# Moving the residual sums, the bias product and the LN2 tails from GpSimd to VectorE in a fused transformer block

## The chip, the core and the metric

The kernel runs on one core of one Trainium2 chip. A core has five engines with a queue of instructions each: PE (TensorE, matrix products into PSUM; PEld stands for its weight loads), DVE (VectorE), ACT (ScalarE), POOL (GpSimd) and SP (SyncE, which here issues the DMAs). Each engine works through its own queue in order and waits, at its head, until semaphores tell that the operands are there and the buffers free. The metric is the time of one execution in microseconds, taken as the median of several runs.

## What is computed

One block with adaptive layer norm: a modulation vector from a condition c, a local attention (16 heads of 28, each query looks at 8 keys, two rows apart), and an MLP. x has 2048 rows of 448 columns, F is 1792.

```python
mod = (silu(c) @ w_mod)                       # sa, ca, ga, sb, cb, gb
h = layernorm(x) * (1 + ca) + sa
x = x + ga * attention(h, wqkv, wo)
h = layernorm(x) * (1 + cb) + sb
y = layernorm(h)                              # the MLP normalises once more
x = x + gb * (gelu(y @ w1 + b1) @ w2 + b2)
```

The last line is what the change is about. The kernel scales w2 by gb once, and computes `x + gb*b2` for each block of rows apart from the product: `gbb2 = gb * b2` (one row, held on all 128 partitions), `x1p = x + gbb2`, and at the end `out = (gelu(...) @ (w2*gb)) + x1p`.

## The kernel before

The rows are cut into 8 blocks (p = 0 to 7) of 256: 128 partitions, and two neighbouring rows on each partition, so a block is a 128 x 896 tile of x. Attention runs in 9 batches (i = 0 to 8) of 228 queries, the MLP in 4 tiles (t = 0 to 3) of two blocks.

The kernel first lists all its operations as numbered tasks (`add`, line 111), each with the engine that does it, and then issues them in an order that is written out by hand: `ORDER` (line 51) holds the task numbers in sequence, with a suffix where a task runs on another engine than its first (`:D` DVE, `:A` ACT, `:P` POOL). A task that goes to an engine is queued there in that sequence. `SLOTS` (line 43) gives each buffer, in the order in which the listing creates them, its place: `P` buffers are the four slots of two PSUM banks each, and a buffer has to wait until all readers of the one before it in its slot are done.

The tasks that the change and the prediction speak of:

- Attention of batch i (line 678): V product `pv` (L706, or L548 for the later batches), its copy on ACT (L721), two logit products `lt` for two halves of the heads (L738), an exponential of each on ACT (L745), a mask product of each on DVE (L751), the sums `pd` (L760) and the attention product `po` (L771), logarithm and exponential of the sums (L780, L782), the output times the inverse sum on DVE (L788).
- q and k of blocks 2 to 7 (line 614): a product `pq` (L548, L554) for k and for q, copied (L628) and transposed by DMA (L631).
- Output projection of block p (line 797): PE product (L803), sum with x on DVE (L810), row statistics (L456, L458), inverse deviation on POOL (`rstd`, L469), normalisation (L478), two products or sums with the modulation (`h2`, L819), statistics again, inverse deviation on POOL again, normalisation to `yb`, and a *tail*: a copy of its last 64 columns per row (L485 to L492) that completes the tile for the DMA transpose `yT` (L834). Tails run on POOL unless ORDER says otherwise: before, those of blocks 0, 3, 4 and 7 run on POOL, 2 and 5 on DVE, 1 and 6 on ACT.
- `gbb2` (L657), on POOL: needs b2, whose load is L368, and gb. The scaling of w2 by gb is seven DVE tasks (L661), one for each pair of 128-row slabs of w2.
- MLP of tile t (line 845): first projection (L548, L554), gelu on ACT (L864), second projection (L883) from the scaled w2, final sum `fin` on DVE (L889), store (L893).
- `residual` (line 838): x1p, two POOL additions per block of 448 columns each (L841), and a *gate* before them (L868): a POOL copy of one element of the first gelu's result, which holds the additions back until that gelu is done.

Around the change, DVE's queue before 74 us holds row statistics and normalisations of blocks 2 and 3 mixed with the seven scalings of w2; the last scaling, of pair 0, is the one whose slab the second projection of tile 0 reads first. POOL's queue holds, in this sequence: inverse deviations, gbb2, an inverse deviation, the gate, the four additions of blocks 0 and 1, the inverse deviation of block 3, its tail. The SP queue holds the load of b2 as its last load but for transposes.

Of the kernel before, what the change touches and what calls it, by code (L numbers as in the profile page):

```python
# [10 lines left out]
BF16 = mybir.dt.bfloat16  # L11
ACT = mybir.ActivationFunctionType
ALU = mybir.AluOpType

S, D, H, DH, F = 2048, 448, 16, 28, 1792
# [5 lines left out]
NS = 2  # L21
# [33 lines left out]
105 119:A 145 143 133 100 146 121 136 134 126 148 137 107 147 7 127 149:D 122 138 124 150 129 139 190 123 191 140 198  # L55
141 128 125 200 199 269 130 271 236 40 270 207 33 209 38 241 201 35 237 208 210 185 211 154 39 153 242 202 152 212
151:A 8 203 187 213 238 204 159 239 214:D 205 215 186 240 155 278 206 188 279 280 156 160 307:R 161 281 243 37 282 272
192 273:A 162 157 189 171 308:D 194 172 283 193 244 218 173 195 163 219 158 275 284 196 216 285 167 217 286 447:P 246
197 164 168 165 228 174 169:D 274 309 312 276:D 277 220 313 310 314 166 221 229 225 230 311 224 222:D 247 170 315 245
176 317 316 175 226 248 233 232 318 227 290 249 289:A 319 43 287:A 223 288 320 234 250 558:P 46 45 559 321 47 231 253  # L60
345 342 346 251 560 303 482:P 44 252 324 343 322 291 561 254 323 325 347 326 344 292 304 255 293 327 348 328 373:R 256
305 294 329 257 350 258 375 52 378 376 330 340:R 53 333 379 235 377 374 296 334 331 300 41 295 351 332 259 49 335 380
299 341 336 337 297 260 382 262 301 381 349 263 261 264 338:A 383 483 352 339 384 265 484 266 449 353 267 485 385 268
# [3 lines left out]
402 452 404 443 487 453 370 490 454 444 436 455 371:D 372 456 434 491 405 488 457 493 445 459 458 492 460 435 494 461  # L67
# [3 lines left out]
513 547 515:D 599 516 564 602 568 481 569 570 604 603 571 546 605 572 548 606 573 628 607 608 574 549 635 575 550 609  # L71
612 636 577 630 637 578 610 629 640 576 579 638 581 639 611 613 580 582 641 631 583 633 586 651 614 632 587 584 585
616 588 642 615 648 617 654 646 647 618 634 652 645 656 621 649 619 644 622 620 623 643 658 650 625 624 589 626 664
590 655 627 591:A 653 657 439 592 659 556 665 662 663 674 666 660 661 669 667 675 668 678 676 679 677 686 672 673 671
687 681 670 680 690 691 694 697 693 682 688 692 685 695 683 689 701 684 698 696 709 699 710 702 711 712 705 700 703
706 704 707 708
# [77 lines left out]
def kernel(  # L154
# [14 lines left out]
    nc = tc.nc  # L169
# [3 lines left out]
    P = Plan()  # L173
    add = P.add

    cst = ctx.enter_context(tc.tile_pool(name="cst", bufs=1))
# [15 lines left out]
    x_all = cst.tile([128, NP, NS * D], BF16, name="x_all")  # L192
# [14 lines left out]
    ga_bc, sb_bc, g2_bc, gb_bc = [mod_bc[:, i, :] for i in range(4)]  # L207
    gbb2_bc = cst.tile([128, D], FP32, name="gbb2_bc")
    seen = cst.tile([128, 1], BF16, name="seen")
    b2_bc = cst.tile([128, D], BF16, name="b2_bc")  # L210
# [160 lines left out]
    for a in range(2):  # L371
        load(lambda a=a: nc.sync.dma_start(out=w1_r[KS * a:KS * a + KS, :],
                                           in_=B_w1[(KT - 1) * 128:D, a * F // 2:(a + 1) * F // 2]), 0.5, [f"w1r{a}"])
    for i in range(7):
        load(lambda i=i: nc.sync.dma_start(out=w2_s[:, 2 * i:2 * i + 2],
                                           in_=B_w2[256 * i:256 * i + 256].rearrange("(f p) n -> p f n", p=128)),
# [105 lines left out]
    def xn(p, n):  # L482
        return x_all[:, p, n * D:(n + 1) * D]

    def tail(zy, keys, key, head=False):  # L485
        src, dst = lambda: zy.t[:, :, DP - 2 * KS:DP - KS], lambda: zy.t[:, :, DP - KS:DP]
        if head:
            add("DVE", 0.11, lambda: nc.vector.tensor_copy(out=dst(), in_=src()), reads=keys, bufs=[zy], writes=[key], name="tail", port=True)
            return
        add("POOL", 0.35, lambda: nc.gpsimd.tensor_copy(out=dst(), in_=src()), reads=keys, bufs=[zy], writes=[key], name="tail",  # L490
            port=True, alt={"DVE": (0.12, lambda: nc.vector.tensor_copy(out=dst(), in_=src())),
                            "ACT": (0.20, lambda: nc.scalar.copy(out=dst(), in_=src()))})  # L492
# [141 lines left out]
    def mods():  # L634
# [22 lines left out]
        add("POOL", 1.05, lambda: nc.gpsimd.tensor_tensor(out=gbb2_bc[:], in0=gb_bc, in1=b2_bc[:], op=ALU.mult),  # L657
# [139 lines left out]
    def out_proj(p):  # L797
# [27 lines left out]
        yb = fixed("zy", zys)  # L825
# [3 lines left out]
        tail(yb, [(yb, 0), (yb, 1)], (yb, 2))  # L829
# [8 lines left out]
    def residual(p, gate):  # L838
        x1p = x1p_of[p] = sb("xp", [128, NS, D], FP32, "x1p")
        for n in range(NS):  # L840
            add("POOL", 1.0, lambda n=n: nc.gpsimd.tensor_tensor(out=x1p.t[:, n, :], in0=xn(p, n), in1=gbb2_bc[:], op=ALU.add),  # L841
                reads=[f"x{p}", "gbb2"], bufs=[x1p], writes=[(x1p, n)], port=True, after=[gate], name="x1p")


    def mlp(t, tbl, lts):
# [22 lines left out]
        gate = add("POOL", 0.1, lambda: nc.gpsimd.tensor_copy(out=seen[:], in_=hm.t[:, 0, 0, 0:1]), reads=[(hm, 0)], bufs=[hm], port=True, name="gate")  # L868
        residual(2 * t, gate)
        residual(2 * t + 1, gate)  # L870
        for q in range(2):
# [5 lines left out]
            for ns, c0, c1 in (([0], 0, D), ([1], 0, D // 2), ([1], D // 2, D)) if last else (([0, 1], 0, D),):  # L877
                p2, n0, n1 = psum("p2"), ns[0], ns[-1] + 1
                for n in ns:
# [11 lines left out]
                    bufs=[p2, x1p], reads=[(p2, n) for n in ns] + [(x1p, n) for n in ns], writes=[f"out{p}{n0}{c0}"] + ([] if last else [f"x{p}"]), name="fin")  # L891
# [71 lines left out]
```

## Time and profile before

| | us |
|---|---|
| median of 3 runs | 169.14 (169.13 to 170.44) |
| span of the profiled execution, first to last instruction | 166.6 |
| DMA share of the slices between 62 and 71 us | 0.9 and more |
| POOL, inverse deviations (22) | 16.7 |
| POOL, gbb2 (1) | 1.1 |
| POOL, gates (4) | 1.3 |
| POOL, tails (7, three of them of the first layer norm) | 2.5 |

How to read the views: a row of a timeline is start, duration, engine, line, operation, output and inputs, shapes and count (rows with a count are several instructions put together); in brackets stands how long the engine had been idle before and what ended that. Times count from the first instruction. "x2" rows of DVE overlap by a few hundredths, since an instruction starts before the one ahead of it has quite ended. In rows of stretches stands for each engine the busy time and the number of instructions, then the granted PE clock, the DMA share and the rate.

### The profile page before, as it was taken

The numbers are of one execution on the slowest core, as the hardware profiler recorded it, in microseconds if no ns is written. First come the engines' busy times: TensorE is split into PE (matmuls) and PEld (weight loads), VectorE is DVE, ScalarE is ACT, GpSimd is POOL, SyncE is SP. The second block draws the span as 40 slices with busy tenths as digits, with TensorE's granted clock in tenths as the row PEclk, the third lists the DMA queues.
The fourth block names the chain that finished last, engine by engine and source line by source line (L and its number), as shares of the span: only waits on it lengthen the run. The fifth ranks groups of instructions, "written<-read, shape, count | busy, mean of one in ns | idle before, by whom it ended". The sixth has DMA issues, their size and how long they took to land.

```text
span 166.6 us, 4971 instructions
## 1 busy us (share of the span) xinstructions
PE 160.9 (97%) x2126; PEld 83.7 (50%) x2126; DVE 116.1 (70%) x271; ACT 102.4 (61%) x142; POOL 46.7 (28%) x73
## 2 busy tenths in 40 slices
PE   6999899999999999999999999999999999999992
PEld 4678544444545543445555344556434455344572
DVE  6889899958899989996938886574788930500032
ACT  3378898798489953859674468947536820097300
POOL 3136332300261201289100114700002870007200
PEclk9999999999999999999999999999999999999999
DMA  5999989799999999900091000009010026110003
GB/s 152 323 335 311 182 269 172 147 160 190 222 185 306 147 161 245 151 0 6 2 139 46 4 0 0 4 0 126 8 55 0 0 55 185 64 46 0 0 1 110
DMA packets 35573, 18.78 MB, mean 113 GB/s; under 512 B 28507, under 2 KB 34592, under 8 KB 35552
## 3 DMA queue, kind: packets, MB, share of 16 engines
q1 hardware_dynamic: 35548, 18.47, 51.0%
q8 instruction: 16, 0.26, 0.7%
q14 instruction: 5, 0.04, 0.1%
q10 hardware_dynamic: 4, 0.00, 0.0%
HBM read 9.81 MB, written 1.84 MB: 70 GB/s over the span
## 4 chain that ended last, share of the span: by engine, by line
PE 88%; DMA 4%; ACT 2%; SPq 2%; POOL 1%; DVE 1%; issue 1%
PE p L883 26%; PE p L548 22%; PE pq L548 8%; PE pw L803 8%; PE pv L706 5%; PE p L554 4%; PE lt L738 4%; PE po L771 3%; PE pv L548 3%; DMA wqk_st<-in_A_wqkv_dram 3%; PE pq L554 2%; DMA kT<-zy 2%; PE pd L760 1%; SPq L349 1%; PE pb L641 1%
## 5 line engine op out<-in xcount | busy, mean ns | idle before, releaser
L864 ACT ACTIVATE hm<-p,b_col 128x512 bf16<-128x512 f32 x56 | 33.9, 692 | 29.9 <-PE p L554 27.3
L883 PE MATMUL p<-w_s,hm 128*128 128x448 bf16 (+1 forms) x238 | 44.1, 342 | 0.0
L548 PE MATMUL p<-yT,w_s 128*128 128x512 bf16 x168 | 38.1, 380 | 0.0
L469 POOL TENSOR_TENSOR rs_all<-mvs,neg_half 128x2 f32<-128x2 f32 x22 | 16.7, 764 | 58.0 <-DVE mvs L458 57.9
L883 PEld LDWEIGHTS <-hm 128*128 128x128 bf16 x238 | 22.6, 98 | 19.3 <-issue 0.8
L889 DVE TENSOR_TENSOR x_all<-p,x1p 128x896 bf16<-128x896 f32 (+2 forms) x10 | 8.9, 902 | 25.9 <-PE p L883 25.9
L548 PEld LDWEIGHTS <-w_s 128*128 128x128 bf16 x168 | 15.8, 98 | 20.9 <-issue 2.9
L456 DVE BATCH_NORM_STATS2 stt<-x_all 128x6 f32<-128x448 bf16 x32 | 18.6, 608 | 0.8 <-DMA x_all<-in_A_x_dram 0.6
L745 ACT ACTIVATE et<-lt 128x928 bf16<-128x928 f32 x18 | 16.0, 947 | 4.2 <-PE lt L738 3.9
L841 POOL TENSOR_TENSOR x1p<-x_all,gbb_bc 128x448 f32<-128x448 bf16 x16 | 17.8, 1137 | 0.0
L548 PE MATMUL pq<-wqk_st,hT 128*128 128x448 bf16 x72 | 15.0, 354 | 0.0
L788 DVE TENSOR_TENSOR qT<-po,den 128x912 bf16<-128x912 f32 x9 | 10.0, 1106 | 6.6 <-ACT den L782 6.4
L751 DVE TENSOR_TENSOR et<-et,mask 128x928 bf16<-128x928 bf16 x18 | 11.8, 683 | 3.1 <-ACT et L745 3.0
L803 PE MATMUL pw<-wo_s,qT 128*128 128x448 bf16 x64 | 13.3, 353 | 0.0
L780 ACT ACTIVATE den<-pd 128x928 f32<-128x928 f32 x9 | 8.5, 943 | 5.9 <-PE pd L760 5.7
L819 DVE TENSOR_TENSOR h<-h,mod_bc 128x896 bf16<-128x896 bf16 x16 | 11.1, 710 | 0.3
L628 ACT CAST zy<-pq 128x896 bf16<-128x896 f32 x10 | 8.9, 912 | 1.7 <-PE pq L554 0.9
L548 PEld LDWEIGHTS <-hT 128*128 128x128 bf16 x72 | 6.4, 98 | 6.9 <-issue 1.6
L782 ACT ACTIVATE den<-den,den_bias 128x928 f32<-128x928 f32 x9 | 9.6, 1072 | 0.2
L478 DVE TENSOR_SCALAR zy<-h,mvs,rs_all 128x448 bf16<-128x448 bf16 x16 | 6.6, 457 | 4.4 <-POOL rs_all L469 4.4
L810 DVE TENSOR_TENSOR x_all<-pw,x_all 128x896 bf16<-128x896 f32 x8 | 8.7, 1086 | 1.3 <-PE pw L803 1.3
L456 DVE BATCH_NORM_STATS2 stt<-h 128x6 f32<-128x448 bf16 x16 | 9.4, 612 | 0.2
(115 smaller groups left out, 182.0 us busy)
## 6 DMA issues: line engine op xcount, KB each, us to landing
w_s<-in_B_w_dram SPq DMA_DIRECT2D x7, 224.0 KB, 3.8
out_dram<-x_all SPq DMA_DIRECT2D x7, 224.0 KB, 2.1
x_all<-in_A_x_dram SPq DMA_DIRECT2D x3, 448.0 KB, 5.3
wmod<-in_w_mod_dram SPq DMA_DIRECT2D x3, 448.0 KB, 7.2
w_s<-in_B_w_dram SPq DMA_DIRECT2D x3, 448.0 KB
wqk_st<-in_A_wqkv_dram SPq DMA_DIRECT2D x3, 225.0 KB, 3.9
wm_st<-in_w_mod_dram SPq DMA_DIRECT2D x1, 672.0 KB, 4.6
x_all<-in_A_x_dram SPq DMA_DIRECT2D x2, 224.0 KB, 2.6
```

What stands on the lines that cost most here:

```text
L456: add("DVE", 0.53, lambda: nc.vector.bn_stats(out=stt[:, w, b, 0:6], in_=src()), reads=reads, bufs=bufs, after=early if w == b == 0 else ( ...
L469: ways = {"POOL": (0.55 + 0.17 * n, lambda: nc.gpsimd.tensor_tensor(out=r, in0=v, in1=neg_half[:, 0:n], op=ALU.pow))}
L548: nc.tensor.matmul(out(), lhsT=lhs(kt, slice(0, 128)), rhs=rhs(kt, slice(0, 128)), start=first and kt == 0, stop=not first and kt == KT - 2)
L554: nc.tensor.matmul(out(), lhsT=lhs(KT - 1, rows), rhs=rhs(KT - 1, rows), start=first, stop=not first, tile_position=(rows.start, 0))
L745: exps.append(add("ACT", 0.83, lambda half=half, lt=lt: nc.scalar.activation(out=et.t[:, 2 * half:2 * half + 2].rearrange("p r m c -> p r ...
L751: nc.vector.tensor_tensor(out=ev, in0=ev, in1=mask[:], op=ALU.mult)
L788: nc.vector.tensor_tensor(out=qT[:, :, LEAD + q00:LEAD + q00 + 2 * WQ], in0=po.t[:, :, 0:NS * 4 * WQ].rearrange("p j (m c) -> p m j c", c=WQ),
L803: nc.tensor.matmul(pw.t[:, s, 0:D], lhsT=qT[:, KT * s + ft, LEAD + 128 * p:LEAD + 128 * p + 128], rhs=wo_s[:, ft, :], start=(ft == 0), sto ...
L819: add("DVE", 0.55, lambda vec=vec, op=op: nc.vector.tensor_tensor(out=h2.t[:], in0=h2.t[:], in1=vec.unsqueeze(1).to_broadcast([128, NS, D] ...
L841: add("POOL", 1.0, lambda n=n: nc.gpsimd.tensor_tensor(out=x1p.t[:, n, :], in0=xn(p, n), in1=gbb2_bc[:], op=ALU.add), reads=[f"x{p}", "gbb ...
L864: gelus.append(add("ACT", 0.585, lambda f=f, a=a, p1=p1s[g]: nc.scalar.activation(out=hm.t[:, f].rearrange("p n c -> p (n c)"), in_=p1.t[: ...
L883: nc.tensor.matmul(p2.t[:, n, 0:c1 - c0], lhsT=hm.t[:, f, n, q * 128:(q + 1) * 128], rhs=w2_s[:, f, c0:c1], start=(f == parts[0][0]), stop ...
```

## The change

Four things move from POOL to DVE, and one is dropped:

- x1p of a block is one DVE addition of 896 columns (gbb2 read twice by a broadcast) instead of two POOL additions of 448;
- gbb2 is a DVE product;
- the tails of the second layer norm that were on POOL (blocks 0, 3, 4, 7) are DVE copies;
- the four gates are gone.

```diff
-    def tail(zy, keys, key, head=False):
+    def tail(zy, keys, key, head=False, late=False):
...
+        if late:
+            add("DVE", 0.12, lambda: nc.vector.tensor_copy(out=dst(), in_=src()), reads=keys, bufs=[zy], writes=[key], name="tail",
+                port=True, alt={"ACT": (0.20, lambda: nc.scalar.copy(out=dst(), in_=src()))})
+            return
...
-        add("POOL", 1.05, lambda: nc.gpsimd.tensor_tensor(out=gbb2_bc[:], in0=gb_bc, in1=b2_bc[:], op=ALU.mult),
+        add("DVE", 0.5, lambda: nc.vector.tensor_tensor(out=gbb2_bc[:], in0=gb_bc, in1=b2_bc[:], op=ALU.mult),
...
-        tail(yb, [(yb, 0), (yb, 1)], (yb, 2))
+        tail(yb, [(yb, 0), (yb, 1)], (yb, 2), late=True)
...
-    def residual(p, gate):
+    def residual(p):
         x1p = x1p_of[p] = sb("xp", [128, NS, D], FP32, "x1p")
-        for n in range(NS):
-            add("POOL", 1.0, lambda n=n: nc.gpsimd.tensor_tensor(out=x1p.t[:, n, :], in0=xn(p, n), in1=gbb2_bc[:], op=ALU.add),
-                reads=[f"x{p}", "gbb2"], bufs=[x1p], writes=[(x1p, n)], port=True, after=[gate], name="x1p")
+        add("DVE", 1.0, lambda: nc.vector.tensor_tensor(out=x1p.t[:], in0=x_all[:, p, :].rearrange("p (s d) -> p s d", s=NS),
+                                                        in1=gbb2_bc[:].unsqueeze(1).to_broadcast([128, NS, D]), op=ALU.add),
+            reads=[f"x{p}", "gbb2"], bufs=[x1p], fills=[x1p], port=True, name="x1p")
...
-        gate = add("POOL", 0.1, lambda: nc.gpsimd.tensor_copy(out=seen[:], in_=hm.t[:, 0, 0, 0:1]), reads=[(hm, 0)], bufs=[hm], port=True, name="gate")
-        residual(2 * t, gate)
-        residual(2 * t + 1, gate)
+        residual(2 * t)
+        residual(2 * t + 1)
```

ORDER and SLOTS are written anew, because the tasks' numbers change and the order between engines with them. Read as queues, PE, ACT and SP have the same tasks in the same sequence as before, and DVE and POOL too, but for the moved ones. These stand in DVE's queue as follows:

| task | place in DVE's queue |
|---|---|
| tail of block 0 | after its normalisation, ahead of the L788 product of batch 4 |
| gbb2 | after the third scaling of w2 and the first statistics of block 2's h2, ahead of block 3's first normalisation; four scalings follow |
| x1p of block 0 | after the seventh scaling, ahead of block 3's first h2 operation |
| x1p of block 1 | after block 3's second h2 operation |
| tail of block 3 | after its normalisation, ahead of the four masks of batches 5 and 6 |
| tail of block 4, x1p of blocks 3 and 2 | after block 4's normalisation, ahead of the first mask of batches 7 and 8 |
| x1p of blocks 5 and 4 | after block 7's first and second h2 sums |
| tail of block 7 | after its normalisation |
| x1p of blocks 6 and 7 | after the final sums of blocks 5 and 4 |

In SLOTS, 25 of 208 buffers follow another buffer than before in their slot; most are swaps of two neighbours. Those that the prediction speaks of: the V product of batch 1 followed block 1's q product and now follows the first logit product of batch 0 (which an exponential reads); block 2's q product followed block 0's q product and now follows the logit products of batch 1 (read by exponentials).

More of the change, by code (lines that the diff above doesn't have):

```diff
@@ L54 @@
 85 90:A 93:P 36 114 94+3@94 82 95 113 102 92:A 91 115:D 86 103 116 96 120:A 144 97 99 104 106 117:A 135 98 118:A 142
[L55 to L63, printed above, removed]
[3 rows of a table removed]
@@ L67 @@
-402 452 404 443 487 453 370 490 454 444 436 455 371:D 372 456 434 491 405 488 457 493 445 459 458 492 460 435 494 461
[3 rows of a table removed]
[L71 to L74, printed above, removed]
@@ L75 @@
-687 681 670 680 690 691 694 697 693 682 688 692 685 695 683 689 701 684 698 696 709 699 710 702 711 712 705 700 703
-706 704 707 708
+105 119:A 145 143 133 100 146 121 136 134 126 137 148 107 147 149:D 7 138 127 150 122 124 139 129 190 123 198 191 140
+200 128 141 125 199 269 271 130 236 270 40 207 33 209 38 201 241 208 210 237 211 185 35 39 242 202 8 187 151:A 238 154
+239 153 152 186 212 159 203 213 188 204 214:D 155 240 215 278 205 279 280 156 160 206 307:R 281 161 243 282 272 192
+273:A 37 157 189 171 162 308:D 194 172 283 193 244 218 173 163 219 195 275 158 284 196 216 167 217 285 246 444:P 197
@@ new lines @@
+286 164 168 165 228 169:D 174 274 309 276:D 312 277 220 313 310 314 166 221 229 225 230 224 311 170 222:D 247 315 245
+176 317 316 175 226 248 233 232 318 227 290 249 289:A 319 287:A 43 234 223 288 320 250 552:P 46 45 553 321 47 231 253
+345 342 346 251 554 303 479:P 252 44 324 343 322 291 254 555 323 325 347 326 344 292 304 255 327 293 348 328 373:R 256
+305 329 294 257 350 258 375 378 52 330 376 340:R 53 333 235 379 377 334 331 374 296 300 332 41 295 259 351 49 335 380
+299 336 341 337 260 297 382 262 381 263 301 261 349 264 338:A 352 480 383 339 384 265 481 266 446 267 353 268 482 385
[9 rows of a table added]
@@ L77 @@
+640 641 612 628 645 639 647 643 615 638 613 649 637 616 614 617 644 619 618 655 583 620 584 621 585:A 648 436 650 586
+656 550 653 654 665 657 651 681 652 660 658 666 682 659 669 667 670 668 677 663 664 662 678 672 661 671 685 673 679
+676 683 674 680 689 675 686 684 697 687 698 690 699 700 693 688 691 694 692 695 696
 """
@@ L208 @@
     gbb2_bc = cst.tile([128, D], FP32, name="gbb2_bc")
-    seen = cst.tile([128, 1], BF16, name="seen")
     b2_bc = cst.tile([128, D], BF16, name="b2_bc")
@@ L890, in mlp @@
                     out=xo(xi), in0=p2.t[:, n0:n1, 0:w], in1=xo(x1p.t), op=ALU.add),
-                    bufs=[p2, x1p], reads=[(p2, n) for n in ns] + [(x1p, n) for n in ns], writes=[f"out{p}{n0}{c0}"] + ([] if last else [f"x{p}"]), name="fin")
+                    bufs=[p2, x1p], reads=[(p2, n) for n in ns], writes=[f"out{p}{n0}{c0}"] + ([] if last else [f"x{p}"]), name="fin")
                 lo, hi = n0 * D + c0, (n1 - 1) * D + c1
```

27 rows, old and new, of tables (ORDER, SLOTS) are left out of this document.

## Prediction

> **What bounds the kernel now.** I read the page first (busy time per engine, chain of work that ended last), then busy time by stretches, then the timelines of PE, DVE, ACT, POOL and SP around each place where an operation is put.
>
> ```profile
> span 166.6 us, 4971 instructions
> PE 160.9 (97%) x2126; PEld 83.7 (50%) x2126; DVE 116.1 (70%) x271; ACT 102.4 (61%) x142; POOL 46.7 (28%) x73
> PE 88%; DMA 4%; ACT 2%; SPq 2%; POOL 1%; DVE 1%; issue 1%
> 22.30:62.00 39.70, 39.29 (x765) 19.52 (x766) 35.64 (x74) 32.34 (x40) 8.45 (x11) 1.00 0.98 191
> 62.00:73.80 11.80, 11.80 (x62) 4.84 (x60) 11.61 (x28) 6.63 (x11) 4.10 (x6) 1.00 0.83 149
> 73.80:163.70 89.90, 89.85 (x992) 45.13 (x990) 49.72 (x94) 49.56 (x70) 25.63 (x31) 1.00 0.18 37
> ```
>
> In the last three rows the columns are stretch, its length, then busy time of PE, PEld, DVE, ACT and POOL. The reader is to see two things. PE is idle 0.41 us between 22.3 and 62, not at all up to 73.8, and 0.05 us in the 89.9 us after that: nothing done elsewhere can win more than half a microsecond there, and any time that PE is made to wait is added to the end in full. And DVE, where the work goes, is busy 11.61 of 11.80 us between 62 and 73.8, but 49.72 of 89.90 after. So the question is whether an operation put into DVE's queue reaches PE, and the dangerous place is before 73.8.
>
> **The buffers, at the start.** The slot list is rewritten too. Nearly all of it is a renaming or a swap of two buffers that come free together; one pair is not. The first V product (batch 1, at 18.07) waited for the buffer that ACT's copy of q reads; it will take the one that the first exponential reads. The first q/k product of block 2 (22.27) had a buffer that was free long before; it will take that of batch 1's second logit product, read by an exponential.
>
> ```profile
> 16.04 1.48 PE L548 MATMUL pq<-hT,Wqk 128*128 128x256 bf16 x12
> 18.07 1.64 PE L706 MATMUL pv<-Wv,hT 128*64 128x448 bf16 x16 [0.55 <-ACT qT L609]
> 21.58 0.70 PE L738 MATMUL lt<-qT,kT 28*64 28x58 bf16 x64
> 22.27 2.44 PE L548 MATMUL pq<-wqk_st,hT 128*128 128x448 bf16 x12
> 16.17 0.94 ACT L745 ACTIVATE et<-lt 128x928 bf16<-128x928 f32 x1 [0.68 <-PE lt L738]
> 17.01 1.01 ACT L609 CAST qT<-pq 128x1024 bf16<-128x1024 f32 x1
> 22.35 0.94 ACT L745 ACTIVATE et<-lt 128x928 bf16<-128x928 f32 x1
> ```
>
> Its reader now ends at 17.11 instead of 18.02, so V starts when PE is free, 17.5, and gains 0.6; the logits end at 21.7 instead of 22.28. Then PE waits for an exponential (0.05 + 0.94 + 0.05) until 22.7, where it went on at 22.27. Net 0.4 us lost. It is not simply added: see the next part.
>
> **gbb2 on DVE.** One product of 128x448 moves from POOL to DVE, directly ahead of the subtraction at 69.40 (block 3's h). Its operand b2 has not come by then.
>
> ```profile
> 65.27 0.95 SPq L368 DMA_DIRECT2D b_bc<-in_B_b_dram  x1
> 70.62 1.13 POOL L657 TENSOR_TENSOR gbb_bc<-mod_bc,b_bc 128x448 f32<-128x448 bf16 x1 [1.25 <-DMA b_bc<-in_B_b_dram]
> w_s<-in_B_w_dram SPq DMA_DIRECT2D x7, 224.0 KB, 3.8
> wmod<-in_w_mod_dram SPq DMA_DIRECT2D x3, 448.0 KB, 7.2
> 69.40 0.40 DVE L478 TENSOR_SCALAR h<-x_all,mvs,rs_all 128x448 bf16<-128x448 bf16 x1
> 69.72 0.62 DVE L456 BATCH_NORM_STATS2 stt<-h 128x6 f32<-128x448 bf16 x1
> 70.25 1.98 DVE L661 TENSOR_TENSOR w_s<-w_s,mod_bc 128x896 bf16<-128x896 bf16 x2
> 72.16 0.25 DVE L458 BATCH_NORM_AGGREGATE mvs<-stt 128x2 f32<-128x9 f32 x2
> 72.33 0.35 DVE L478 TENSOR_SCALAR h<-x_all,mvs,rs_all 128x448 bf16<-128x448 bf16 x1
> 72.60 1.15 DVE L661 TENSOR_TENSOR w_s<-w_s,mod_bc 128x896 bf16<-128x896 bf16 x2
> 73.67 2.00 DVE L819 TENSOR_TENSOR h<-h,mod_bc 128x896 bf16<-128x896 bf16 x2
> 73.80 3.19 PE L883 MATMUL p<-w_s,hm 128*128 128x448 bf16 x16
> ```
>
> POOL waited for b2 until 70.62 and nobody minded. DVE will stand there from 69.4 to about 70.6, and behind it in its queue are four scalings of w2. The last of them (pair 0) ended at 72.60 + 1.15 = 73.75, and the second projection's first matmul, which reads pair 0, started at 73.80: no slack. From gbb2's start G on, by differences of starts: gbb2 0.53 (as the 448-wide statistics, 69.72 to 70.25; bounds 0.3 by the rate of the 896-wide bf16 scalings, 1.13 by POOL's), then 0.32 + 0.53 + 1.07 + 0.17 + 0.27 + 1.07 = 3.43, where I take 1.07 (73.67 - 72.60) for the first pair of scalings too, because its 1.98 fell beside POOL's product and POOL will be idle; 0.08 to the end of the last, 0.05 to PE. So PE starts at G + 4.09. With G = 70.6 that is 74.69, 0.9 us late. PE itself arrives 0.4 late from the buffers, so that loss is inside this one. G: the load's issue moves by the 0.4 of the start and back by about 0.2 for the first tail (below); I take 70.6 as it was. Bounds: at the 3.8 us of the w2 loads b2 is there before DVE asks (G = 69.8, loss 0.4, that of the buffers alone); at the 7.2 us of the modulation loads G is 72.5 (loss 2.8).
>
> **x1p on DVE, before the logits' masks.** Sixteen POOL additions of 448 columns become eight DVE additions of 896.
>
> ```profile
> 65.81 1.27 DVE L819 TENSOR_TENSOR h<-h,mod_bc 128x896 bf16<-128x896 bf16 x2
> 73.75 4.85 POOL L841 TENSOR_TENSOR x1p<-x_all,gbb_bc 128x448 f32<-128x448 bf16 x4
> 76.98 0.73 DVE L478 TENSOR_SCALAR zy<-h,mvs,rs_all 128x448 bf16<-128x448 bf16 x1
> 79.29 0.70 DVE L478 TENSOR_SCALAR zy<-h,mvs,rs_all 128x448 bf16<-128x448 bf16 x2 [1.49 <-POOL rs_all L469]
> 80.46 0.39 DVE L478 TENSOR_SCALAR zy<-h,mvs,rs_all 128x448 bf16<-128x448 bf16 x1
> 80.77 1.09 DVE L889 TENSOR_TENSOR x_all<-p,x1p 128x896 bf16<-128x896 f32 x1
> 81.77 0.19 DVE L491 COPY zy<-zy 128x128 bf16<-128x128 bf16 x1
> 81.87 1.74 DVE L751 TENSOR_TENSOR et<-et,mask 128x928 bf16<-128x928 bf16 x3
> 83.91 1.39 PE L771 MATMUL po<-et,vb 64*32 64x57 bf16 x128
> 133.96 1.32 DVE L478 TENSOR_SCALAR zy<-h,mvs,rs_all 128x448 bf16<-128x448 bf16 x4 [0.81 <-POOL rs_all L469]
> ```
>
> The nearest row to the new addition is the final one (L889): as many columns, an fp32 operand, 80.77 to 81.77 = 1.00 us from start to start. Bounds: 0.54 at the pace of the bf16 scalings, 1.09 at that row's whole length. I take 1.00. From the h2 product (73.67) to the end of the last mask (81.87 + 1.74 = 83.61) DVE needed 9.94 us. Added: two additions, 2.0, and a tail with its wait, 0.2. Gone: the slowing of DVE beside POOL's additions (2.00 - 1.27 = 0.73 and 0.73 - 0.39 = 0.34), and half of the wait for the inverse deviation, which had queued on POOL behind those additions (1.49 becomes the 0.81 of the later row). 10.38 us, begun at G + 3.96 = 74.56, end at 84.94. PE's attention product needs that mask and arrives at 83.91 + 0.89 = 84.80: another 0.15 to 0.2 us. Sum so far 1.05; with the bounds 0.9 (DVE is then early) and 1.25.
>
> The Trainium skill (VectorE: DVE Perf Modes, on fp32 tensor_tensor) gives (N+151)/0.96 ns, 1.09 us for 896 columns. By it this part would cost 0.2 us more and the time would be 170.3; the row's 1.00 is from start to start, which is what the queue pays.
>
> **The rest.** Tails: four copies of 0.19 us leave POOL; the first falls into a DVE wait ahead of batch 4's output product (L788). The gates go without trace, since nothing on POOL is left behind them. Blocks 2 and 3:
>
> ```profile
> L841 POOL TENSOR_TENSOR x1p<-x_all,gbb_bc 128x448 f32<-128x448 bf16 x16 | 17.8, 1137 | 0.0
> 107.78 1.45 DVE L751 TENSOR_TENSOR et<-et,mask 128x928 bf16<-128x928 bf16 x1 [1.46 <-ACT et L745]
> 137.04 1.30 SPq L834 DMA_TRANSPOSE yT<-zy  x1
> 141.86 2.75 PE L548 MATMUL p<-yT,w_s 128*128 128x512 bf16 x12
> DMA to landing us min/median/max: 3.1/3.2/4.4
> ```
>
> DVE idles 1.46 us there and its mask loses the 0.8 us that POOL cost it, so two additions of 1.0 fit. Blocks 4 and 5: 2.0 us of additions less 0.7 of slowing put the last transpose from 137.04 to about 138.3; it lands 3.2 later, 141.5, and PE asks for it at 141.86 + 1.05: covered, though by no more than 1.4 us. Blocks 6 and 7 lie in DVE's idle time near the end. Nothing is won by POOL's 17.8 us, because no PE wait hung on them.
>
> **Sum.** 166.6 + 1.0 = 167.6 us of span. The runs' median, 169.14, is 2.5 us above the profiled span; that part I leave as it is: 170.1 us, 0.6% slower. A measurement of this kernel can tell about 1%, so this counts as the same.
>
> **Rivals.** (a) b2 comes in time or PE catches up, and only the buffers' loss or nothing remains: 169.0 to 169.5. For it: DVE recovers 0.8 us per collision with POOL. Against: G would have to be below 69.8, with the load's wait in the row. Chance 0.12. (b) PE's fullness is only apparent, and it absorbs the late start: 169.1. Against: 16 matmuls of 448 columns take 3.19 us, as dense as everywhere, with no idle row. Chance 0.05. The Trainium skill (Perfetto Trace Analysis, Identifying the Most-Contended Engine) says that matmul busy time is no good measure of headroom and names weight-load time instead, here 50%; by that rule (b) would hold. (c) b2 comes later, at 7.2 us after issue, or DVE's queue stays behind through the transposes of blocks 4 and 5 (from 1.4 us of extra delay on): 170.9 to 172.2. It decides from G = 71.4. Chance 0.21. (d) Faster: POOL's collisions held DVE, DVE held PE. DVE wins back 0.73 + 0.34 + 0.69 in the stretch above and about 0.8 near 107.78, but PE's idle time there is 0.05 us; at most the 0.41 us before 62 is to be had, 168.7. A gain of over 1%, under 167.4, has no row for it. Chance 0.03.
>
> **How the numbers follow.** My forecast, 169.6 to 170.8, has 0.59; with (a) and (b) the same side of 1% has 0.76, (c) is the slower 0.21, (d) the faster 0.03. The range of 8 in 10 takes in (a) down to 169.2 and (c) up to 171.3.
>
> **What would show it.** Right: DVE's gbb2 starts near 70.6 with a wait on b2's load; the first second-projection matmul starts near 74.7 with an idle PE before it; batch 6's attention product near 85.0; PE idle about 0.05 us from there on; V at 17.5 and block 2's q/k product at 22.7. Wrong: gbb2 without a wait; an addition far from 1.0 us; idle PE behind 86, above all before the last first projection.

## The result, and the profile after

| | before | after |
|---|---|---|
| median in the first comparison, us (4 runs each) | 169.79 | 171.61 |
| ratio, 95% interval | | 1.0122, 1.0078 to 1.0165 |
| span of the profiled execution, us | 166.63 | 169.63 |
| first projection (L548, after L550) starts | 62.80 | 64.24 |
| b2 lands (where DVE waits for it, gbb2 starts 0.02 later: G) | 70.49 | 72.18 |
| second projection (L883, after L884) starts | 73.80 | 76.30 |
| from the first projection's start to the last product's end | 100.85 | 101.90 |
| from there to the end of the span | 2.99 | 3.49 |

The change made the kernel slower, by more than forecast: 171.61 stands outside the range that ended at 171.3. Three further comparisons, each on another chip, gave 1.0065 (1.0033 to 1.0098), 1.0109 (1.0063 to 1.0155) and 1.0067 (1.0031 to 1.0102). The four ratios are on average 1.0091, about 1.5 us. Some executions of either kernel fall into a slower state; ratios and intervals are of the others alone, medians are of all, so a ratio is not the quotient of two medians. Line numbers of after are one or two off those of before.

The page of after, its totals, and three groups (busy time and mean ns, then idle time ahead of them):

```profile
span 169.6 us, 4944 instructions
PE 162.5 (96%) x2126; PEld 84.9 (50%) x2126; DVE 120.9 (71%) x284; ACT 102.3 (60%) x142; POOL 28.4 (17%) x48
L884 PE MATMUL p<-w_s,hm 128*128 128x448 bf16 (+1 forms) x238 | 44.1, 342 | 1.0 <-DVE w_s L663 1.0
L550 PE MATMUL pq<-wqk_st,hT 128*128 128x448 bf16 x72 | 15.0, 353 | 1.1 <-ACT et L747 1.1
L842 DVE TENSOR_TENSOR x1p<-x_all,gbb_bc 128x896 f32<-128x896 bf16 x8 | 8.5, 1084 | 0.0
```

POOL gave up 18.3 us of work and DVE took on 4.8; neither figure shows in the time. Two waits of PE do: 1.0 us ahead of the second projection and 1.1 us ahead of a q/k product. Where the first comes from stands in the timeline of after: the load on SP, DVE's queue between 70 and 77 us, then PE:

```profile
66.78 0.57 SPq L366 DMA_DIRECT2D b_bc<-in_B_b_dram  x1
70.18 0.62 DVE L454 BATCH_NORM_STATS2 stt<-h 128x6 f32<-128x448 bf16 x1
72.20 0.62 DVE L659 TENSOR_TENSOR gbb_bc<-mod_bc,b_bc 128x448 f32<-128x448 bf16 x1 [1.40 <-DMA b_bc<-in_B_b_dram]
72.74 0.39 DVE L476 TENSOR_SCALAR h<-x_all,mvs,rs_all 128x448 bf16<-128x448 bf16 x1
73.05 0.62 DVE L454 BATCH_NORM_STATS2 stt<-h 128x6 f32<-128x448 bf16 x1
73.59 1.15 DVE L663 TENSOR_TENSOR w_s<-w_s,mod_bc 128x896 bf16<-128x896 bf16 x2
74.65 0.26 DVE L456 BATCH_NORM_AGGREGATE mvs<-stt 128x2 f32<-128x9 f32 x2
74.82 0.36 DVE L476 TENSOR_SCALAR h<-x_all,mvs,rs_all 128x448 bf16<-128x448 bf16 x1
75.09 1.16 DVE L663 TENSOR_TENSOR w_s<-w_s,mod_bc 128x896 bf16<-128x896 bf16 x2
76.16 1.09 DVE L842 TENSOR_TENSOR x1p<-x_all,gbb_bc 128x896 f32<-128x896 bf16 x1
...
74.48 0.82 PE L556 MATMUL p<-yT,w_r 64*128 64x512 bf16 x6
76.30 1.86 PE L884 MATMUL p<-w_s,hm 128*128 128x448 bf16 x9 [1.00 <-DVE w_s L663]
```

The reader is to see one unbroken line: the load is issued at 66.78, DVE stands idle for 1.40 us until it lands, gbb2 starts at 72.20, and the four scalings queued behind it end at 75.09 + 1.16 = 76.25. PE was done at 75.30 and starts at 76.30. That is G + 4.10; the prediction had G + 4.09.

PE is full from there on, as before. Stretches of after (cut at the second projection) and, below them, of before:

```profile
64.24:76.30 12.06, 11.06 (x57) 4.55 (x56) 10.55 (x27) 6.91 (x12) 2.97 (x3) 1.00 0.74 131
76.30:166.15 89.85, 89.84 (x990) 45.08 (x989) 54.59 (x104) 48.66 (x68) 8.30 (x10) 1.00 0.19 37
```

```profile
62.80:73.80 11.00, 11.00 (x57) 4.45 (x56) 10.85 (x26) 5.85 (x10) 4.10 (x6) 1.00 0.81 145
73.80:163.65 89.85, 89.85 (x992) 45.13 (x990) 49.70 (x93) 49.56 (x70) 25.63 (x31) 1.00 0.18 37
```

The second stretch is 89.85 us in both, so the eight additions and the tails cost PE nothing there in the end. The profiled spans differ by 3.00 us: 1.44 before the first projection, 1.06 up to the second, and 0.50 behind the last product. The 1.44 us are no more than two executions of one kernel differ by, as the first experiments show.

### The profile page after: what moved, and what is told of

It reads as the page before. It is cut to its first block, busy times and chain, and to the rows that moved or that the text cites. A ratio compares the mean times of both kernels' runs of the same rounds, so it can differ in the third digit from the quotient of the medians.

```text
span 169.6 us, 4944 instructions
## 1 busy us (share of the span) xinstructions
PE 162.5 (96%) x2126; PEld 84.9 (50%) x2126; DVE 120.9 (71%) x284; ACT 102.3 (60%) x142; POOL 28.4 (17%) x48
## 4 chain that ended last, share of the span: by engine, by line
PE 69%; DVE 9%; ACT 7%; DMA 6%; SPq 4%; issue 2%; POOL 1%; DVEq 0%; POOLq 0%
PE p L884 25%; PE p L550 16%; PE pw L805 5%; PE pq L550 4%; DMA b_bc<-in_B_b_dram 3%; PE p L556 3%; DMA mod_bc<-mod_hbm 3%; PE pv L708 3%; PE lt L740 2%; ACT den L784 2%; ACT zy L630 2%; PE ps_c L380 2%; ACT et L747 2%; SPq L633 2%; DVE stt L454 2%
## 5 line engine op out<-in xcount | busy, mean ns | idle before, releaser
L884 PE MATMUL p<-w_s,hm 128*128 128x448 bf16 (+1 forms) x238 | 44.1, 342 | 1.0 <-DVE w_s L663 1.0
L550 PE MATMUL p<-yT,w_s 128*128 128x512 bf16 x168 | 38.1, 379 | 0.0
L467 POOL TENSOR_TENSOR rs_all<-mvs,neg_half 128x2 f32<-128x2 f32 x22 | 19.2, 878 | 82.3 <-DVE mvs L456 82.2
L884 PEld LDWEIGHTS <-hm 128*128 128x128 bf16 x238 | 22.7, 98 | 20.2 <-issue 1.8
L550 PEld LDWEIGHTS <-w_s 128*128 128x128 bf16 x168 | 15.8, 98 | 20.9 <-issue 2.9
L550 PE MATMUL pq<-wqk_st,hT 128*128 128x448 bf16 x72 | 15.0, 353 | 1.1 <-ACT et L747 1.1
L753 DVE TENSOR_TENSOR et<-et,mask 128x928 bf16<-128x928 bf16 x18 | 10.8, 628 | 2.0 <-ACT et L747 2.0
L550 PEld LDWEIGHTS <-hT 128*128 128x128 bf16 x72 | 6.5, 97 | 8.0 <-issue 1.7
L821 DVE TENSOR_TENSOR h<-h,mod_bc 128x896 bf16<-128x896 bf16 x16 | 9.7, 619 | 0.3
L805 PEld LDWEIGHTS <-qT 128*128 128x128 bf16 x64 | 5.9, 98 | 6.7 <-DVE qT L790 1.4
L842 DVE TENSOR_TENSOR x1p<-x_all,gbb_bc 128x896 f32<-128x896 bf16 x8 | 8.5, 1084 | 0.0
```

The source lines that it names most:

```text
L467: ways = {"POOL": (0.55 + 0.17 * n, lambda: nc.gpsimd.tensor_tensor(out=r, in0=v, in1=neg_half[:, 0:n], op=ALU.pow))}
L550: nc.tensor.matmul(out(), lhsT=lhs(kt, slice(0, 128)), rhs=rhs(kt, slice(0, 128)), start=first and kt == 0, stop=not first and kt == KT - 2)
L753: nc.vector.tensor_tensor(out=ev, in0=ev, in1=mask[:], op=ALU.mult)
L805: nc.tensor.matmul(pw.t[:, s, 0:D], lhsT=qT[:, KT * s + ft, LEAD + 128 * p:LEAD + 128 * p + 128], rhs=wo_s[:, ft, :], start=(ft == 0), sto ...
L821: add("DVE", 0.55, lambda vec=vec, op=op: nc.vector.tensor_tensor(out=h2.t[:], in0=h2.t[:], in1=vec.unsqueeze(1).to_broadcast([128, NS, D] ...
L884: nc.tensor.matmul(p2.t[:, n, 0:c1 - c0], lhsT=hm.t[:, f, n, q * 128:(q + 1) * 128], rhs=w2_s[:, f, c0:c1], start=(f == parts[0][0]), stop ...
```

## The experiments

The theory at first: the wait for b2 is the whole loss. The rivals: the buffers, the additions, or something ahead of the first projection. Each kernel below is timed against the kernel before on the same chip. Where an expectation speaks of the sum or the bias "of block 2", it means gbb2 and b2, the bias of the second projection; block 2 of the rows has no part in them.

**The same two kernels again.** The changed kernel (three more times) and the kernel before.

> The changed kernel as it is, once more. Theory 1 (gbb2 stands in DVE's queue until b2 has landed, and the second projection of tile 0 waits for the scalings behind it; the exchanged buffers at the start lose another 0.5 us): the same two PE waits as in the first profile of the change, 1.0 to 1.1 us ahead of block 2's q/k product near 23 us and 1.0 to 1.2 us ahead of the second projection near 76 us; ratio to before 1.008 to 1.012. Rival (the greater part of the 3.0 us between the two profiled spans is the late release of PE's clock, at 10.9 us instead of 5.6 us in the profile of before, which differs from one execution to the next): a profile whose warm-up products come 0.11 us apart from 5.6 us on has a span near 168.5, one with the late release near 169.6.

> The changed kernel once more, against the kernel before on another chip. Theory (the change costs the wait of 0.8 to 1.0 us ahead of the second projection and next to nothing else): ratio 1.005 to 1.008, and from the first projection's start to the last product 101.7 to 102.0 us. Rival (the first comparison, 1.012, has the true size, from further losses ahead of the first projection): ratio 1.010 or more.

> The changed kernel once more on the chip of the three others. Theory (a wait of 0.8 to 1.0 us and 0.48 us in the closing part): 1.3 to 1.5 us slower than before, ratio 1.007 to 1.010. Rival (the wait alone): ratio 1.006 or less.

> The kernel before, unchanged. Theory (the prediction's base was a fast execution): ratio 1.000 within 0.003, and a profile whose first projection starts near 63.5 to 64 us, not 62.80, with a span of 167.5 to 168.5 us; the time near 170.2. Rival (the first profile was an ordinary execution, and the change moves the first projection): the first projection starts at 62.8 within 0.2 and the span is 166.6 within 0.3 again.

The ratios of the changed kernel stand above: after_again (1.0065) and after_fourth (1.0067) came out below what was expected of them, after_third (1.0109) above, and the intervals overlap throughout. The kernel before came out at 1.000 (0.9957 to 1.0042), and its new profile shows what the first one was: span 168.16 instead of 166.63, first projection at 64.29 instead of 62.80 (63.5 to 64 was expected). The difference arises ahead of 31 us. DVE in the timeline of the second profile of before:

```profile
30.78 0.40 DVE L478 TENSOR_SCALAR zy<-x_all,mvs,rs_all 128x448 bf16<-128x448 bf16 x1 [1.85 <-DMA zT<-zy]
```

and in the first, on which the prediction was built:

```profile
28.28 0.40 DVE L478 TENSOR_SCALAR zy<-x_all,mvs,rs_all 128x448 bf16<-128x448 bf16 x1
```

The same instruction waits 1.85 us for a transpose in the one and not at all in the other. Of all the profiles of this study only that first one has its first projection ahead of 63.2; the others lie between 63.3 and 66.0 us, with old and new buffers alike. The first profile was of a quick execution. Its own time is not on record, but it can be estimated: in each of the 19 other profiles the execution's time stands 1.70 or 1.71 us above its span, so this one took about 166.63 + 1.71 = 168.3 us, 0.8 less than the median of 169.14 that the prediction set beside it.

The rival named in the first of these expectations, PE's pace at the start, does show in the first profile of after. The same nine warm-up products, in before and then in after:

```profile
8.31 1.14 PE L382 MATMUL pq<-warm_w 128*128 128x256 bf16 x9
8.85 2.02 PE L380 MATMUL pq<-warm_w 128*128 128x256 bf16 x9
```

In after such products begin 0.21 us apart until 10.7 us, in before 0.11 us apart from 5.7 us on, and the first product of q begins 1.42 us later (10.71 instead of 9.29). But an early quick pace does not make the short span that the rival expected: after_again has it from 6.1 us on, with a span of 168.96, and after_third from 5.9 us on, with 169.41.

**gbb2 alone: later, alone in the old kernel, and with an earlier load.** gbb2_late moves one task in `ORDER` of the changed kernel, 177 (gbb2), from ahead of block 3's first normalisation to directly ahead of block 0's x1p, behind all scalings:

```diff
-... 419 177 412 393 ... 368 179 178 429 ...
+... 419 412 393 ... 368 179 178 177 429 ...
```

before_gbb2 changes the kernel before in gbb2 alone; b2_early moves the load (task 42) ahead of the last four loads of w2 in SP's queue.

```diff
-        add("POOL", 1.05, lambda: nc.gpsimd.tensor_tensor(out=gbb2_bc[:], in0=gb_bc, in1=b2_bc[:], op=ALU.mult),
+        add("DVE", 0.5, lambda: nc.vector.tensor_tensor(out=gbb2_bc[:], in0=gb_bc, in1=b2_bc[:], op=ALU.mult),
```

> The changed kernel with gbb2 four scalings later in DVE's queue, directly ahead of block 0's residual sum. Theory 1: no PE wait ahead of the second projection of tile 0, 1.0 to 1.2 us less than the changed kernel, ratio to before 1.000 to 1.006. Rival (the eight additions and four tails on DVE make it late whatever gbb2 does): the wait ahead of the second projection or of the attention product near 86 us remains, less than 0.3 us won.

> The kernel before with one edit: the sum of residual and scaled bias of block 2 on VectorE, at the place in its queue that the change gives it. Theory (the wait for block 2's bias is the whole of the change's loss): TensorE waits 0.7 to 1.0 us ahead of the second projection, which starts 4.1 us after that load has landed; ratio 1.004 to 1.007. Rival (the other moved operations make the loss): no wait there, ratio 1.000 within 0.003.

> The changed kernel with the load of block 2's bias issued ahead of the last four loads of the second projection's weights. Theory: it lands before VectorE reaches the sum, the second projection starts with no wait over 0.2 us, ratio 1.000 to 1.003 against before. Rival (the weights that are now loaded later, or the extra work on VectorE itself, hold the projection): a wait of 0.5 us or more remains, ratio 1.004 or more.

Measured: gbb2_late 1.0002 (0.996 to 1.0043), before_gbb2 1.0049 (1.0014 to 1.0084), b2_early 1.0005 (0.9968 to 1.0043). Timeline of gbb2_late, DVE and PE:

```profile
73.28 1.16 DVE L663 TENSOR_TENSOR w_s<-w_s,mod_bc 128x896 bf16<-128x896 bf16 x2
74.35 0.62 DVE L659 TENSOR_TENSOR gbb_bc<-mod_bc,b_bc 128x448 f32<-128x448 bf16 x1
75.00 1.09 DVE L842 TENSOR_TENSOR x1p<-x_all,gbb_bc 128x896 f32<-128x896 bf16 x1
...
74.79 0.59 PE L556 MATMUL p<-yT,w_r 64*128 64x512 bf16 x4
75.32 3.20 PE L884 MATMUL p<-w_s,hm 128*128 128x448 bf16 x16
```

and of before_gbb2:

```profile
71.34 0.63 DVE L657 TENSOR_TENSOR gbb_bc<-mod_bc,b_bc 128x448 f32<-128x448 bf16 x1 [1.28 <-DMA b_bc<-in_B_b_dram]
...
75.44 0.73 PE L883 MATMUL p<-w_s,hm 128*128 128x448 bf16 x3 [0.87 <-DVE w_s L661]
```

and of b2_early:

```profile
63.29 0.57 SPq L366 DMA_DIRECT2D b_bc<-in_B_b_dram  x1
71.06 0.60 DVE L659 TENSOR_TENSOR gbb_bc<-mod_bc,b_bc 128x448 f32<-128x448 bf16 x1
...
74.83 0.82 PE L556 MATMUL p<-yT,w_r 64*128 64x512 bf16 x6
75.58 1.69 PE L884 MATMUL p<-w_s,hm 128*128 128x448 bf16 x8
```

With gbb2 behind the scalings they end at 74.44 and PE passes from one projection to the next without a wait. With gbb2 alone moved in the old kernel the wait is there. With the load issued at 63.29, DVE's gbb2 runs at 71.06 with no wait, and PE goes straight on too. In the profiles that bear on it (us from the first projection's start to the last product's end; from the load's landing to the second projection's start):

| kernel | first projection to last product | landing to second projection |
|---|---|---|
| before, before_again | 100.85, 100.89 | 3.31, 3.05 |
| gbb2_late, b2_early | 100.84, 100.97 | 3.32, load early |
| after, after_again, after_third | 101.90, 101.85, 101.72 | 4.12, 4.13, 4.12 |
| before_gbb2 | 101.77 | 4.12 |

So the place of gbb2 costs 0.8 to 1.0 us, and by itself it makes the whole difference in this stretch. The theory holds for it. The wait does not depend on how late an execution runs: in all 19 profiles with the load in its old place b2 lands 7.4 to 8.1 us behind the first projection's start. The second projection could start 11.0 us behind it; gbb2 and the scalings, which take 4.1 us from the landing, are done later than that.

**The buffers.** old_slots and late_old_slots put the `SLOTS` list of before into the changed kernel and into gbb2_late; before_new_slots and new_slots_again put the new list into the kernel before; nothing else differs.

> The changed kernel with the buffer places of the kernel before. Theory 1: no PE wait ahead of block 2's q/k product (1.0 us less there), V of batch 1 waits 0.6 us again, so 0.4 to 0.5 us less up to there; the load of b2 goes out earlier by as much, so 0.4 to 0.5 us less in all. Rival (the SP queue or the modulation row's way through HBM sets b2's load, not PE): the start is 0.45 us shorter, the wait ahead of the second projection longer by as much, total unchanged within 0.2 us.

> Both edits: gbb2 behind the scalings and the buffer places of the kernel before. Theory 1: neither of the two waits; what is left of the change (eight additions, four tails on DVE, no gates) costs nothing, ratio to before 0.997 to 1.002. Rival (the additions on DVE cost time of their own): ratio over 1.003 with a PE wait behind 73 us.

> The kernel before with the change's numbers of buffers alone. Theory: the first V product starts about 0.6 us earlier and block 2's q/k product about 1.1 us after that is lost, and the wait ahead of the scaled output weights' first product takes up the difference: ratio 0.998 to 1.003. Rival (the buffers cost as predicted): 0.4 to 0.5 us more, ratio 1.003.

> The changed kernel with the buffer numbers of before. Theory (the buffers' gain and loss are absorbed by later waits on loads): the same time as the changed kernel beside it within 0.4 us. Rival (the buffers cost 0.4 to 0.5 us, as predicted): 0.4 us or more shorter than it.

> The kernel before with the change's buffer numbers alone. Theory (absorbed): ratio 0.997 to 1.003. Rival (they cost 0.4 us or more): ratio 1.003 or more, the first run of this edit gave 1.0063.

Measured: old_slots 1.0117 (1.0055 to 1.0178) beside 1.0065 for the changed kernel on that chip, old_slots_again 1.0113 (1.0047 to 1.0178) beside 1.0109, late_old_slots 1.0012 (0.9972 to 1.0052) beside 1.0002, the new list in the old kernel 1.0063 (1.0019 to 1.0107) and then 1.0016 (0.9982 to 1.0049). Taking the new list away did not help, and putting it in showed a loss the first time, against the expectation, and none clear of zero the second, so neither a loss nor a gain of the whole is shown. What it does at its own place is plain in the timeline of new_slots_again:

```profile
17.43 1.64 PE L706 MATMUL pv<-Wv,hT 128*64 128x448 bf16 x16
22.71 1.48 PE L548 MATMUL pq<-wqk_st,hT 128*128 128x448 bf16 x7 [1.06 <-ACT et L745]
```

V at 17.43 and block 2's q/k product at 22.71 are the 17.5 and 22.7 of the prediction: 0.4 us are lost here. Whether they reach the end stays open; the first projection starts at 62.8 to 64.7 us in the six profiles with the old list and at 63.3 to 66.0 in the fourteen with the new, and varies by more than 0.4 us between executions of one kernel.

**Twice the additions.** gbb2_late with every x1p addition issued twice, which doubles its cost and leaves the computed values as they are.

```diff
+        def twice():
+            for _ in range(2):
+                nc.vector.tensor_tensor(out=x1p.t[:], ...)
-        add("DVE", 1.0, lambda: nc.vector.tensor_tensor(out=x1p.t[:], ...),
+        add("DVE", 2.0, twice,
```

> The changed kernel with block 2's sum late in VectorE's queue (as in gbb2_late) and with each addition of x1p issued twice, the second with the same result. Theory (the additions lie in VectorE's queue ahead of the last masks, with 0.07 us of slack before batch 6's attention product): that product starts 1.5 to 2 us later against the end of the first tile's second projection, and the time is 1.5 to 2.5 us longer, ratio 1.010 to 1.016. Rival (the additions lie in idle time of VectorE): within 0.3 us, ratio 1.000 to 1.003.

Measured: 1.0261 (1.0201 to 1.0321), more than expected. Waits of PE from 76 us on in x1p_twice (total, times, longest):

```profile
PE p L550 <- DMA yT<-zy: 1.1, 1, 1.1
PE pd L762 <- DVE et L753: 0.9, 1, 0.9
PE po L773 <- DVE et L753: 0.7, 1, 0.7
```

From the second projection's start to batch 6's attention product it took 12.30 us instead of gbb2_late's 10.11, so the two further additions of 1.1 us each are paid there in full: this place has no slack. Then PE waited 1.1 us for the last transpose, whose input DVE makes behind the additions of blocks 4 and 5: the second mechanism of rival (c), though what is transposed there belongs to blocks 6 and 7. Together 3.3 us of 4.4; another 0.5 lies behind the last product (below), and the first projection started late, at 65.02. The additions of the change itself just fit; the doubled ones do not.

**The last half microsecond.** A loss was left that no theory had: behind the last product, every profile of a kernel with the whole change and no filling takes 3.46 to 3.49 us to the end of the span, every one without it (before_gbb2 and the kernel before with the new buffer list among them) 2.98 to 3.00. The transfers of the last 13 us (packets, MB, share of 16 engines) in after, and then in before:

```profile
q1 hardware_dynamic: 576, 0.46, 10.6%
q14 instruction: 2, 0.02, 0.5%
```

```profile
q1 hardware_dynamic: 576, 0.46, 10.6%
```

After fetches two blocks of instructions there, before none. So the number of instructions of POOL (108 in the trace of before, 73 after, with those that don't count as busy) and of DVE (308, and 321) was changed by small stores into a scratch tile, in idle time: 35 on POOL behind its last operation, 35 on DVE behind its last addition, or both; late_pool_fill and late_both_fill have gbb2 late besides.

```diff
     P.emit(filler)
+    for _ in range(35):
+        nc.gpsimd.memset(fill[:], 0.0)
```

> The changed kernel with 35 one-column stores on GpSimd behind its last operation (about 137 us), so that GpSimd's program is as long as before; they write a scratch tile and nothing waits for them. Theory (from the last product's end to the end of the span the changed kernel takes 3.47 us where before took 2.99, because GpSimd's shorter program leaves instruction fetches to the very end): 2.99 to 3.05 us again, no instruction packet in the last 10 us, and 0.4 to 0.5 us less than the changed kernel. Rival (GpSimd's length has nothing to do with it): 3.45 us or more.

> The changed kernel with 35 one-column stores on VectorE behind the last x1p addition, in its idle time near 150 us. Theory (GpSimd's program length sets the closing part): it stays at 3.45 to 3.50 us. Rival (VectorE's program length sets it): 2.99 to 3.05 us.

> Both repairs: block 2's sum late in VectorE's queue, and the 35 stores on GpSimd. Theory: no wait ahead of the second projection, closing part of 2.99 to 3.05 us, ratio 0.996 to 1.000 against before. Rival (a third loss remains): ratio 1.003 or more.

> The changed kernel with both fillings, 35 small stores on GpSimd and 35 on VectorE, in idle time. Theory (each of the two engines holds the closing barrier for an instruction fetch of its own, GpSimd until 3.47 us and VectorE until 3.29 us after the last product): 2.99 to 3.05 us, no instruction packet in the last 10 us. Rival (one of the two is not cured by length): 3.28 us or more.

> The same with block 2's sum late in VectorE's queue: both repairs in full. Theory: no wait ahead of the second projection, closing part 2.99 to 3.05 us, ratio 0.996 to 1.000. Rival (GpSimd's relief is worth time once the repairs are in): ratio 0.995 or less.

At the end all engines meet in a barrier. A DRAIN is an instruction of the program's end there. The table has, from the last product's end, when the last DRAIN of DVE and the next to last of POOL ended in the trace (us), when the span ended, and the instruction blocks fetched there:

| kernel | POOL's | DVE's | end of span | blocks | ratio, interval |
|---|---|---|---|---|---|
| before | 2.57 | 2.59 | 2.99 | 0 | |
| after | 3.06 | 3.07 | 3.49 | 2 | |
| pool_fill | 2.58 | 3.07 | 3.29 | 1 | 1.0053, 1.0016 to 1.0089 |
| dve_fill | 3.04 | 2.59 | 3.47 | 1 | 1.0111, 1.0065 to 1.0156 |
| both_fill | 2.57 | 2.59 | 2.99 | 0 | 1.0122, 1.0066 to 1.0178 |
| late_pool_fill | 2.56 | 3.06 | 3.28 | 1 | 1.0004, 0.9967 to 1.0041 |
| late_both_fill | 2.57 | 2.59 | 2.99 | 0 | 1.0024, 0.9984 to 1.0063 |
| x1p_twice | 3.06 | 2.59 | 3.48 | 1 | |

Each engine comes 0.5 us late, or on time, by the length of its own program, and for each engine that is late one block is fetched at the end; filling one alone leaves the other to hold the barrier. On DVE six more instructions suffice: x1p_twice has 327 instead of 321, and its DRAIN is on time. It is not that a shorter program is later, since before has 308.

How the length does it is not shown. It is not the arrival of those blocks: their packets start 3.5 to 3.9 us behind the last product, when the late DRAINs (3.07 at most) and the span itself are over. In after, no instruction is recorded on POOL from 168.58 to 169.00 us and none on DVE from 168.63 to 169.08, ahead of their DRAINs, and the packets start at 169.70 and 169.75. In before the same pauses last 0.07 and 0.09 us.

So the expectation of pool_fill and late_pool_fill (2.99 to 3.05) was half wrong: DVE held them at 3.28 and 3.29. This shows in the traces, not in the medians: both_fill, which has 0.5 us less than after by its trace, measured no less. With intervals of 0.4 to 0.6% either way half a microsecond is too little for these comparisons. With both losses taken away late_both_fill is at 1.0024, above its expectation (0.996 to 1.000), with an interval that takes in 1. No kernel here beats before.

## Why the prediction was wrong, point by point

- *PE is full from 62 us on, and a wait of PE is added to the end in full.* Right: 89.85 us behind the second projection's start in both kernels, and with a wait of 0.75 to 1.00 us ahead of it the time from the first projection to the last product is 101.65 to 101.96 us instead of 100.84 to 100.98 (x1p_twice left out, which has other waits). Rival (b), that PE's fullness is only apparent, falls. Its ground was weight-load time, 50%, as the measure of headroom. The Trainium skill (Perfetto Trace Analysis, Identifying the Most-Contended Engine) names that measure beside MFU, the share of the peak rate that the products reach. No view here gives MFU; weight-load time taken alone misled in this case.
- *Buffers: V at 17.5, q/k at 22.7, 0.4 us net.* Right at the place, where PE starts at its usual pace; in the first profile of after both came 1.0 us later, 18.50 and 23.77, with the same wait of 1.06 us. Not settled for the end.
- *gbb2 waits for b2; PE at G + 4.09; 0.9 us late.* Right in the mechanism and in G + 4.09: 4.09 or 4.10 behind gbb2's start in every profile in which DVE waits for b2 there (4.11 to 4.13 behind the landing). The 0.9 us are right partly by luck. The prediction let 0.4 of them be PE's own late arrival, which leaves a wait of 0.5 us; the waits were 0.75 to 1.00 us, since the load goes out and lands with PE's progress (7.4 to 8.1 us behind the first projection's start), so what PE loses earlier does not shorten the wait. G was 72.20 instead of 70.6 for the same reason: the whole execution ran later by then, and b2 took 5.4 us from issue to landing against 5.2. G lies past the 71.4 of rival (c), and the median of 171.61 lies inside (c)'s 170.9 to 172.2, but neither of (c)'s ways led there: b2 did not take 7.2 us, and PE did not wait for the last transposes in after. Nor did (a) or (d) come about: gbb2 had its wait on b2, and PE had no time to win back.
- *x1p 1.00 us from start to start, another 0.15 to 0.2 us.* The 1.00 is right: 76.16 to 77.17 in after. Batch 6's attention product comes 10.21 us behind the second projection's start, 10.11 in before, so 0.10 more; but the 89.85 us say that it was made up later and did not reach the end. By the Trainium skill (VectorE: DVE Perf Modes) an addition takes 1.09 us. The profile's 1.084 agrees as the length of one, and the queue paid 1.01.
- *The gates go without trace, nothing is won or lost by POOL; 166.6 + 1.0.* This is the step that failed: the sum has no term for the stretch behind the last product, which it put at nothing without a row or a bound. With POOL's shorter and DVE's changed program that stretch took 3.47 to 3.49 us instead of 2.99, so 0.48 to 0.50 us were missing; the filled kernels show that the programs' lengths make them, and by what way stays open.
- *"The runs' median, 169.14 ...: 170.1 us".* The sum's base failed too. What is added up here comes to 169.14 + 1.0, and 169.14, a median of three runs, was low: the same kernel had 169.79 in the comparison that decided, and medians of 169.6 to 170.2 over 11 to 35 runs. The 2.5 us between median and span were no fixed part either (about 1.7 are, and about 0.8 came from the profile of a quick execution), but that did not make the forecast too low: with 1.7 instead it would have been 169.3.

So the sum of 1.0 us for what the change does lacked 0.48, and its base was 0.65 too low; that makes 1.1 of the 1.5 us that were missed (171.61 less 170.1). The remaining 0.4 us is less than the 0.7 us by which the first comparison itself is uncertain either way, and its cause stays open. The forecast that this would count as no change (0.76) rested on the short sum: at 1.0 + 0.48 us the loss is 0.9%, which is also the average of the four comparisons, on the edge of what was called the same.

## What to carry to other kernels

Before an operation is moved into a busy engine's queue, look for what it has to wait for: a product of 0.6 us that nobody waited for on an idle engine cost 0.8 to 1.0 us where four operations of the critical path stood behind it, and cost nothing behind them, or with its load issued some 3.5 us earlier. A forecast of a time rests on the base that it adds to: let the range take in how far medians of few runs move, and find out whether the profile was of a quick execution before times of its rows are compared with another's. And what happens behind the last product belongs to the sum too: here the length of two engines' programs moved the end by half a microsecond.

## What the runs showed of the hardware

- On one queue (q14) instructions came in packets of 8 KB during the run. In every kernel in which such packets start behind the last product (3.5 to 3.9 us behind it), as many engines had come to their DRAIN 0.5 us late; without one, both came on time. The Trainium skill (Runtime: NRT & Kernel Launch, Instruction fetch mechanics) has each sequencer fetch the next block while it runs the present one and calls the cost of a block's boundary "mostly hidden". Up to the last product that agrees with the traces: in after a block came at 87.5 us, and PE was busy 89.84 of the 89.85 us around it. Whether the half microsecond at the end is the cost of such a boundary is not shown.
- One inverse deviation of two columns on POOL took 3.35 us in after; the median of the 22 there is 0.70 us, and before has none over 0.98:

```profile
74.99 3.35 POOL L467 TENSOR_TENSOR rs_all<-mvs,neg_half 128x2 f32<-128x2 f32 x1 [4.18 <-DVE mvs L456]
```

  It ran beside two scalings, the first x1p and two h2 products on DVE, back to back from 75.09 to 78.4, all with two operands in SBUF, and ended at 78.34, as the next x1p began (78.36). The Trainium skill (SBUF — State Buffer, Who interferes with whom) says that such DVE instructions contend with a POOL instruction that reads SBUF, and that the order of issue decides which of the two is blocked. The trace fits the contention, though no experiment was made on it; it does not show the order plainly, since POOL's row starts 0.10 us ahead of the first scaling. In before it was DVE that was stretched beside POOL's additions. Nothing on PE waited for it here.
